# Third and fourth q tiles, and one layer norm, turned by VectorE instead of TensorE

## The chip, the cores and the metric

The kernel runs on one core of a Trainium2 chip. TensorE (PE) multiplies matrices, VectorE (DVE), ScalarE (ACT) and GpSimd (POOL) work on tiles of up to 128 partitions, SyncE (SP) issues the DMA transfers. A tile lies in SBUF; matmuls write to banks of PSUM. The metric is the device time of one execution in microseconds (us), the median of several runs.

## The reference

A transformer block whose layer norms are modulated by a condition `c`, with linear attention and a bilinear FFN. S = 2048 tokens, D = 512, F = 1376, 32 heads of 16:

```python
mod = (silu(c) @ w_mod).reshape(6, D)            # sa, ca, ga, sb, cb, gb
h = layernorm(x) * (1 + ca) + sa
q, k, v = split(h @ wqkv)                        # 32 heads of 16
phi = lambda t: where(t > 0, t + 1, exp(t)) + 1e-6
kv = sum over tokens of phi(k) (x) v             # one 16x16 matrix per head
z = sum over tokens of phi(k)
o = (phi(q) @ kv) / (phi(q) . z + 1e-6)
x = x + ga * (o @ wo)
h = layernorm(x) * (1 + cb) + sb
x = x + gb * (((h @ w_gate) * (h @ w_up)) @ w_down)
```

## The kernel before

The 2048 tokens are four chunks of four tiles of 128 tokens, so tile i is tile j = i mod 4 of chunk i div 4. Every product of fp32 matrices is three matmuls of a shorter type: each operand is split into a high part (ACT copies it) and a low part (the rest, a subtraction on DVE or POOL), and high·high, high·low and low·high are summed in PSUM (`product`, L207 to L209). `split` does this for one tile, `split_raw` for a weight.

The first phase loads the inputs and runs over the 16 tiles with a step i for each: norms, products with the key weights, the sum z and the sum over tokens of x and phi(k). A table `extra` hangs other work on these steps: at steps 4 to 7 the four splits of the value weights, at steps 14 and 15 the splits of the output weight `wo`. Then 48 small matmuls of 128x128 make the key-value matrix, and `w_out` multiplies it with `wo`, so that attention and output projection become one matrix of 512 x 512, the four pairs `wp`.

For a q tile the kernel computes phi(q) with tokens on partitions (`q_a`, `q_b`), its denominators (`den_p` the product with z, `den_r` the sum over a head, `den_b` the constant and the reciprocal for a chunk), and scales phi(q) by them (`den_c`, L700). For the product with `wp` the tile has to be turned, so that features are on partitions. Two ways are in use:

- tiles 0 to 3: `turn_a` (L771), four TensorE transposes of 128x128 into PSUM;
- tiles in `FLIPPED` (4 to 15): their columns are held in another order; `move_out` writes the tile to DRAM, `move_in` reads it back with four DMAs that move blocks of 32 rows, and `turn_v` (L802) turns 32x32 blocks with one VectorE instruction, STREAM_TRANSPOSE.

Both end with `turn_h` (L775, the high part on ACT) and `turn_l` (L779, the low part `xl` on DVE). Then `y_step(i)` runs: TensorE transposes of the next tile if it is turned that way, 12 matmuls of tile i (L832) onto a PSUM bank that ACT seeded with x (`y_seed`, L823), the parts of tile i + 1, the sums for the second norm of tile i − 1 (`y_b`, L250 and L251), and whatever else the call hands it.

When a chunk's four tiles have their y, its second layer norm follows: `rstd_of` (`ve` on DVE, L260; the power on POOL, L263), `nmr_of` (DVE, L267), `xhat` (ACT, L272: the tiles n), and for chunks 0 and 1 `ln2_turn`: 16 TensorE transposes (L293) and the modulation with its parts (L305 to L316). The first norms of some chunks are turned through DRAM and VectorE: `lift_out` (L324), `lift_in` (L332, four DMAs per tile), `lift_turn` (L336), `lift_row` (L341, the modulation), `lift_parts` (L349 to L352).

The FFN's F is cut into 11 slices. The last three, f0, f1 and f2 (f2 is 96 wide), are computed plainly per chunk for chunks 0 and 1: `gate_up` (L915 to L917; its second half multiplies the two and splits the product), `down` (L941 to L943), and `evac` (L902), which adds the result to x. Their weights are loaded by `load_ffn`, nine DMAs issued by SP behind the loop over the q tiles, and prepared by `scale_down` (L882), `split_gu` and `split_down`. The other slices go through `ffn`, which is not touched.

The order of the code is the order of each engine's instructions (`manual_schedule`), and SP's queue holds its DMAs in code order too. SBUF has 94 tile buffers that are used again when a tile is done with, PSUM two pools of four banks.

Of the kernel before, what the change touches and what calls it, by code (L numbers as in the profile page):

```python
# [9 lines left out]
F32R = mybir.dt.float32r  # L10
# [4 lines left out]
P = 128  # L15
# [9 lines left out]
def tile_adaln_block(  # L25
# [51 lines left out]
    def B(tag, shape=(P, D), dt=F32):  # L77

        return T(tiles, tag, shape, dt)
# [4 lines left out]
    def bank():  # L84
        return T(ps_w, "bank")
# [100 lines left out]
    def mod_row(v, pair):  # L186
        ps = row_sum(pair)
        t = consts.tile([P, D], F32, name=f"row{v}")
        nc.scalar.activation(t, ps, AF.Copy)
        return t  # L190


    def split(src, h, l, low=None):
        nc.scalar.activation(h, src, AF.Copy)  # L194
        (low or nc.vector).tensor_tensor(l, src, f32(h), op=ALU.subtract)  # L195

    def split_raw(raw, shape=(P, D), low=None):
        h = B("w", shape, F32R)
        l = B("w", shape, F32R)
        split(raw, h[:raw.shape[0]], l[:raw.shape[0]], low)  # L200
        return h, l

    def product(ps, pairs):

        n = len(pairs)
        for i, ((ah, al), (bh, bl)) in enumerate(pairs):
            nc.tensor.matmul(ps, ah, bh, start=i == 0, stop=False)  # L207
            nc.tensor.matmul(ps, ah, bl, start=False, stop=False)  # L208
            nc.tensor.matmul(ps, al, bh, start=False, stop=i == n - 1)  # L209

    def cut(pair, a, b):
        return pair[0][:, a:b], pair[1][:, a:b]

    FLIPPED = range(4, NCH * NJ)

    def by_block(x):
        return x.rearrange("p (s q i) -> p q s i", q=NQ, i=BL)
# [327 lines left out]
    def mod_part(v, *ks):  # L545
        if 0 in ks:
            accs[v] = B("f")
        mod_acc(accs[v], raw_m[v], ks)

    extra = {4: lambda: (wv.extend(split_raw(r) for r in raw_v[0:1]),),  # L550
             5: lambda: (wv.extend(split_raw(r) for r in raw_v[1:2]),),
             6: lambda: (wv.extend(split_raw(r) for r in raw_v[2:3]), mod_load(2),),
             7: lambda: (wv.extend(split_raw(r) for r in raw_v[3:4]),),
# [3 lines left out]
             11: lambda: (mod_part(3, 3), mod_part(4, 0, 1), rows.update({2: mod_row(2, pairs[2])}), raw_o.extend(load(wo_v[k], "raw") for k in range(2, KD))),  # L557
             12: lambda: (mod_part(4, 2, 3), cols.update({3: col_out(3, mod_col(accs[3], bank()), 0.0)}), mod_load(5)),
             13: lambda: (mod_part(5, 0, 1, 2), cols.update({4: col_out(4, mod_col(accs[4], bank()), 1.0)})),
             14: lambda: (mod_part(5, 3), wo_s.extend(split_raw(x) for x in raw_o[:2])),  # L560
             15: lambda: wo_s.extend(split_raw(x) for x in raw_o[2:])}
    pairs = {}
    q_at = {3: 0, 4: 1, 6: 2, 7: 3, 10: 4}
    ahead = {2: k_ps[2], 3: k_ps[3]}
# [102 lines left out]
    def den_z():  # L667

        nc.vector.reduce_sum(den0, zb.rearrange("p (h i) -> p h i", i=DH), axis=AX.X)
        nc.vector.tensor_scalar(den0, den0, EPS_PHI, EPS_DEN, op0=ALU.mult, op1=ALU.add)  # L670
        nc.vector.tensor_copy(den0q.rearrange("p (q s h) -> p q s h", q=NQ, s=KD),
                              den0.rearrange("p (s q h) -> p q s h", q=NQ, s=KD))

    def den_p(ch, *js, on=None):
        for j in js:
            pzs[ch, j] = B("f")
            (on or nc.gpsimd).tensor_tensor(pzs[ch, j], phq[ch * NJ + j], zq if ch * NJ + j in FLIPPED else zb, op=ALU.mult)
# [12 lines left out]

    def den_b(ch):
        nc.vector.tensor_tensor(dens[ch], dens[ch], (den0q if ch * NJ in FLIPPED else den0).unsqueeze(1).to_broadcast([P, NJ, NH]), op=ALU.add)
        nc.vector.reciprocal(dens[ch], dens[ch])

    def den_c(*tiles):

        for i in tiles:
            ch, j = divmod(i, NJ)
            p3 = phq[i].rearrange("p (h i) -> p h i", i=DH)
            nc.vector.scalar_tensor_tensor(p3, p3, EPS_PHI, dens[ch][:, j].unsqueeze(2).to_broadcast([P, NH, DH]),  # L700
                                           op0=ALU.add, op1=ALU.mult)

    def q_tile(i):
        q_a(i, proj(i, wq))

    wp = []
# [36 lines left out]
    kvp = (B("xh", dt=F32R), B("xl", dt=F32R))  # L743
    kvf = B("n")
    nc.vector.tensor_tensor(kvf.rearrange("p (g c) -> p g c", g=KD), kvps.rearrange("p (g c) -> p g c", g=KD),
                            mask.unsqueeze(1).to_broadcast([P, KD, P]), op=ALU.mult)
    den_p(0, 2, on=nc.vector)
    split(kvf, *kvp)
    den_r(0, 2)
    den_a(0, 3, on=nc.vector)  # L750
    den_b(0)
    q_a(8, ps)
    ps = proj(9, wq)
    q_b(8)
    w_out(0, 1)
    q_a(9, ps)
    den_c(0)
    w_out(2, 3)
    q_b(9)
    q_tile(10)  # L760


    pqs = {}

# [24 lines left out]
    def move_out(*tiles):  # L789

        for i in tiles:
            moved[i] = lift_out(f"moved_{i}", phq.pop(i))
# [17 lines left out]
    def ready(*tiles):  # L810
        den_c(*tiles)
        move_out(*tiles)

    y_banks = []

# [448 lines left out]
    def fill(n):  # L1264
        for _ in range(n):
# [2 lines left out]
    f0, f1, f2 = lone  # L1268
    turn_a(0)
    ps = proj(11, wq)  # L1270
    den_c(1)
    turn_h(0)
    turn_l(0)
    y_seed(0)
    den_c(2)
    q_a(11, ps)
    q_b(10)
    y_step(0, lambda: den_c(3), lambda: q_b(11))
    y_step(1, lambda: den_a(1, 0, on=nc.vector))
    y_step(2, lambda: split_gu(f0, nc.gpsimd))  # L1280
    den_a(1, 1, on=nc.vector)
    y_step(3, lambda: scale_down(f0), turn=False, seed=False)
# [15 lines left out]
    split_down(f0, nc.gpsimd)  # L1298
    ready(7)
    move_in(5)  # L1300
    ln2_turn(0, 0, 1, cast=nc.vector)
    q_b(13)
    ps15 = proj(15, wq, acc_bank)
# [27 lines left out]
    turn_v(7)  # L1331
    g()
    den_a(2, 2, on=nc.vector)
    y_step(5, lambda: den_a(2, 3, on=nc.vector))
    y_step(6, lambda: den_b(2), lambda: ready(8))
    y_step(7, lambda: ready(9), lambda: move_in(8), turn=False, seed=False)
    y_b(7)
    norm2[1].rstd_of()
    ready(10)
    ln2_nx(1)  # L1340
# [152 lines left out]
```

## Time and profile before

| | us |
|---|---|
| runs | 552.09, 552.14, 553.29; median 552.14 |
| profiled execution | 551.79 |
| span of the profiled execution | 550.1 |
| TensorE busy | 544.3 |
| VectorE busy | 378.8 |
| ScalarE busy | 294.2 |
| GpSimd busy | 203.5 |

The span is cut into instructions and DMA transfers, all timed from its start; the 1.7 us between execution and span lie outside it. In a row of the timeline stand the start, the duration, the engine, the line of the kernel, the operation, the tile that it writes, those that it reads, and their shapes; `x4` is a group of four. Brackets give the idle time of the engine before the row, and what ended it. Matmuls overlap, so the start of one to the start of the next is its cost, not its duration.

The work around the change lies in these stretches: the 48 small products from 131.57, the first y step from 151.88, the second norm of chunk 0 from 167.52, gate and up of f0 to f2 with y steps 4 to 7 between 176 and 204, and the down product, the second norm of chunk 1 and y steps 8 and 9 from 204.24 to 219.82.

### The profile page before, as it was taken

The page shows a single profiled execution, that of the slowest core. Times are in us where ns is not written, and L with a number is a line of the kernel's source. Part 1 is how long each engine was busy: PE and PEld are TensorE (multiplying, and loading weights), DVE is VectorE, ACT ScalarE, POOL GpSimd, SP SyncE. Part 2 cuts the span into 40 slices and gives each one's busy share as a digit, 9 for nine tenths or more (in the row PEclk, how much of TensorE's full clock was granted, in tenths as well). Part 3 has the DMA queues.
Part 4 walks back from the last instruction along what each step waited for, and adds up shares of the span by engine and source line. Part 5 has one row for each costly group of instructions (what it writes and reads, how often), then busy time and mean ns, then how long its engine had stood idle before and what let it go on. Part 6 is the DMA issues. An engine that isn't in the chain of part 4 may idle for free.

```text
span 550.1 us, 7373 instructions
## 1 busy us (share of the span) xinstructions
PE 544.3 (99%) x2456; PEld 445.7 (81%) x2456; DVE 378.8 (69%) x618; ACT 294.2 (53%) x543; POOL 203.5 (37%) x206
## 2 busy tenths in 40 slices
PE   8999999999999999999999999999999999999997
PEld 7788788888888878878888888877888888888886
DVE  7897779989987876869766576985444344434444
ACT  3695777647577667467674545454443444444210
POOL 2001010001021200066696566766666646446100
PEclk9999999999999999999999999999999999999999
DMA  8903427310504215755454071790344222200004
GB/s 286 385 17 105 126 98 210 101 53 3 157 1 166 64 38 180 243 165 132 145 133 136 19 212 38 245 295 15 120 135 116 58 57 57 59 19 1 0 1 153
DMA packets 64134, 62.48 MB, mean 114 GB/s; under 512 B 7969, under 2 KB 43041, under 8 KB 64097
## 3 DMA queue, kind: packets, MB, share of 16 engines
q1 hardware_dynamic: 64096, 62.02, 36.4%
q8 instruction: 19, 0.31, 0.2%
q14 instruction: 19, 0.15, 0.1%
HBM read 44.70 MB, written 17.30 MB: 113 GB/s over the span
## 4 chain that ended last, share of the span: by engine, by line
PE 97%; DVE 1%; ACT 0%; issue 0%; DVEq 0%
PE bank L1091 33%; PE acc L832 7%; PE acc L1171 6%; PE acc L1173 6%; PE acc L1172 6%; PE bank L209 5%; PE bank L207 4%; PE bank L208 4%; PE acc L416 3%; PE acc L414 3%; PE acc L415 2%; PE bank L917 2%; PE bank L915 2%; PE bank L916 2%; PE acc L146 2%; PE acc L942 1%
## 5 line engine op out<-in xcount | busy, mean ns | idle before, releaser
L1091 PE MATMUL bank<-h,w 128*128 128x512 f32 (+1 forms) x798 | 184.7, 390 | 0.0
L1091 PEld LDWEIGHTS bank<-h,w 128*128 128x128 f32 (+1 forms) x798 | 148.4, 186 | 33.3 <-ACT bank L1096 0.6
L1096 ACT ACTIVATE bank<-bank 128x512 f32<-128x512 f32 (+1 forms) x38 | 22.2, 583 | 139.6 <-PE bank L1091 139.5
L902 DVE TENSOR_TENSOR x<-acc,x 128x512 f32<-128x512 f32 (+1 forms) x73 | 48.5, 680 | 48.3 <-PE acc L1173 47.7
L1077 POOL TENSOR_TENSOR w<-raw,w 128x256 fp32r<-128x256 f32 (+3 forms) x38 | 40.7, 1071 | 91.8 <-ACT w L1070 91.8
L1171 PE MATMUL acc<-w,kh 128*128 128x512 f32 (+2 forms) x154 | 59.6, 387 | 0.0
L1172 PE MATMUL acc<-w,kh 128*128 128x512 f32 (+2 forms) x154 | 59.6, 387 | 0.0
L1173 PE MATMUL acc<-w,kl 128*128 128x512 f32 (+2 forms) x154 | 59.5, 386 | 0.0
L263 POOL TENSOR_TENSOR rstd<-ve,half 128x2 f32<-128x2 f32 (+1 forms) x12 | 11.7, 978 | 119.3 <-DVE ve L262 66.8
L195 POOL TENSOR_TENSOR w<-raw,w 128x512 fp32r<-128x512 f32 (+1 forms) x25 | 35.0, 1404 | 52.8 <-ACT w L194 52.8
L1077 POOL TENSOR_TENSOR w<-t,w 128x512 fp32r<-128x512 f32 (+1 forms) x38 | 49.2, 1313 | 0.0
L195 DVE TENSOR_TENSOR kl<-u,kh 128x512 fp32r<-128x512 f32 (+1 forms) x38 | 26.4, 735 | 30.5 <-ACT kh L194 30.5
L207 PE MATMUL bank<-w,h 128*128 128x512 f32 x104 | 40.9, 394 | 0.0
L209 PE MATMUL bank<-w,h 128*128 128x512 f32 x104 | 40.9, 393 | 0.0
L208 PE MATMUL bank<-w,h 128*128 128x512 f32 x104 | 40.6, 390 | 0.0
L832 PE MATMUL acc<-w,xh 128*128 128x512 f32 x120 | 37.4, 393 | 0.0
L1150 DVE TENSOR_TENSOR u<-bank,u 128x512 f32<-128x512 f32 (+1 forms) x19 | 13.1, 691 | 31.6 <-PE bank L1091 23.9
L1171 PEld LDWEIGHTS acc<-w,kh 128*128 128x128 f32 (+1 forms) x154 | 28.9, 188 | 6.0
L1172 PEld LDWEIGHTS acc<-w,kh 128*128 128x128 f32 (+1 forms) x154 | 28.9, 188 | 5.9
L1173 PEld LDWEIGHTS acc<-w,kl 128*128 128x128 f32 (+1 forms) x154 | 28.9, 188 | 5.9
L1059 POOL TENSOR_TENSOR t<-raw,t 128x256 f32<-128x256 f32 (+1 forms) x34 | 26.1, 768 | 1.3
L832 PEld LDWEIGHTS acc<-w,xh 128*128 128x128 f32 x120 | 22.2, 188 | 4.6
(216 smaller groups left out, 1115.6 us busy)
## 6 DMA issues: line engine op xcount, KB each, us to landing
raw<-in_w_mod_dram SPq DMA_DIRECT2D x24, 256.0 KB, 3.6
raw<-in_B_w_down_dram SPq DMA_DIRECT2D x20, 256.0 KB, 3.0
raw<-in_B_w_gate_dram SPq DMA_DIRECT2D x36, 128.0 KB, 3.4
raw<-in_B_w_up_dram SPq DMA_DIRECT2D x36, 128.0 KB, 3.6
x<-in_A_x_dram SPq DMA_DIRECT2D x16, 256.0 KB, 5.4
out_dram<-x SPq DMA_DIRECT2D x15, 256.0 KB, 2.7
raw<-in_A_wqkv_dram SPq DMA_DIRECT2D x12, 256.0 KB, 5.4
moved<-h SPq DMA_DIRECT2D x12, 256.0 KB, 2.1
```

The source lines that it names most:

```text
L195: (low or nc.vector).tensor_tensor(l, src, f32(h), op=ALU.subtract)
L207: nc.tensor.matmul(ps, ah, bh, start=i == 0, stop=False)
L208: nc.tensor.matmul(ps, ah, bl, start=False, stop=False)
L209: nc.tensor.matmul(ps, al, bh, start=False, stop=i == n - 1)
L832: nc.tensor.matmul(yps[i], x, y, start=False, stop=k == KD - 1 and x is al, skip_group_check=True)
L902: nc.vector.tensor_tensor(xt[:, a:b], dn[j][:, a:b], xt[:, a:b], op=ALU.add)
L1059: sub = lambda out, x, y: (on or nc.gpsimd).tensor_tensor(out, x, y, op=ALU.subtract)
L1077: sub = lambda out, x, y: (on or nc.gpsimd).tensor_tensor(out, x, f32(y), op=ALU.subtract)
L1091: mm = lambda x, y, **kw: nc.tensor.matmul(ps, x[:, k], y, skip_group_check=True, **kw)
L1171: nc.tensor.matmul(ps, hh[:, a:b], dh[:n, c:d], start=i == 0, stop=False)
L1172: nc.tensor.matmul(ps, hh[:, a:b], dl[:n, c:d], start=False, stop=False)
L1173: nc.tensor.matmul(ps, hl[:, a:b], dh[:n, c:d], start=False, stop=i == len(hs) - 1)
```

## The change

- `FLIPPED` begins at tile 2: tiles 2 and 3 of chunk 0 are held in the other column order, written to DRAM and read back (two DMAs out, eight in), and turned by STREAM_TRANSPOSE; their eight TensorE transposes go. `den_b` takes a part of a chunk, as the two halves of chunk 0 now have constants in different orders. The scalings `den_c` of tiles 2, 3 and 1 are moved ahead of q tile 10 and of the first turn; all ten DMAs stand on SP's queue ahead of the nine loads of `load_ffn`.
- The second norm of chunk 1 goes through DRAM: `xhat_blocks`, four DMAs out and 16 in, four `lift_turn`, four `lift_row` and `lift_parts`, instead of 16 TensorE transposes and `ln2_turn`. `rstd_of` and `nmr_of` come in two parts, for tiles 0 to 2 and for tile 3.
- Y steps 5, 6 and 7 follow y step 4 directly; before, gate and up of f2 stood between 4 and 5. `down(0)` takes f0 and f1 first and f2 after. The low part of f2's down weight is made by POOL.
- Denominators of chunks 2 and 3 come sooner: those of tiles 8 and 9 before the second norm of chunk 0 is turned, those of chunk 3 spread over the stretch up to gate and up of f0 in chunk 1.
- One split of a value weight comes at step 3 instead of 4, and all four splits of `wo` at step 14.

```diff
-    FLIPPED = range(4, NCH * NJ)
+    FLIPPED = range(2, NCH * NJ)
...
-    extra = {4: lambda: (wv.extend(split_raw(r) for r in raw_v[0:1]),),
+    extra = {3: lambda: (wv.extend(split_raw(r) for r in raw_v[0:1]),),
...
-             14: lambda: (mod_part(5, 3), wo_s.extend(split_raw(x) for x in raw_o[:2])),
-             15: lambda: wo_s.extend(split_raw(x) for x in raw_o[2:])}
+             14: lambda: (mod_part(5, 3), wo_s.extend(split_raw(x) for x in raw_o))}
...
-    den_b(0)
+    den_b(0, 0, 2)
+    den_b(0, 2, 4)
...
     den_c(0)
+    ready(2)
+    move_in(2)
     w_out(2, 3)
+    ready(3)
+    den_c(1)
+    move_in(3)
     q_b(9)
     q_tile(10)
...
-    den_c(1)
     turn_h(0)
     turn_l(0)
     y_seed(0)
-    den_c(2)
     q_a(11, ps)
     q_b(10)
-    y_step(0, lambda: den_c(3), lambda: q_b(11))
+    y_step(0, lambda: q_b(11))
+    turn_v(2)
     y_step(1, lambda: den_a(1, 0, on=nc.vector))
+    turn_v(3)
     y_step(2, lambda: split_gu(f0, nc.gpsimd))
...
+    den_a(2, 0, 1, on=nc.vector)
     ln2_turn(0, 0, 1, cast=nc.vector)
...
     g = gate_up(0, f1)
     turn_v(6)
-    den_a(2, 0, on=nc.vector)
+    turn_h(5)
+    turn_l(5)
+    y_seed(5)
     split_down(f1, nc.gpsimd)
     g()
-    y_step(4, lambda: scale_down(f2), lambda: den_a(2, 1, on=nc.vector))
-    g = gate_up(0, f2)
-    split_down(f2)
+    y_step(4, lambda: turn_v(7))
     turn_h(6)
     turn_l(6)
-    y_seed(6)
-    turn_v(7)
+    den_b(2, 0, 2)
+    ready(8, 9)
+    move_in(8, 9)
+    y_step(5, lambda: scale_down(f2))
+    y_step(6, lambda: den_a(2, 2, 3, on=nc.vector))
+    y_step(7, turn=False, seed=False)
+    den_b(2, 2, 4)
+    g = gate_up(0, f2)
+    norm2[1].rstd_of(0, 3)
+    y_b(7)
+    ready(10)
+    norm2[1].nmr_of(0, 3)
+    norm2[1].rstd_of(3, 4)
+    norm2[1].xhat_blocks(0, 1, 2)
+    lifts = [lift_out(f"second_1_{n}", norm2[1].n[n]) for n in range(3)]
+    ready(11)
+    norm2[1].nmr_of(3, 4)
+    norm2[1].xhat_blocks(3)
+    lifts.append(lift_out("second_1_3", norm2[1].n[3]))
+    lifts = [lift_in(x) for x in lifts]
+    move_in(10, 11)
+    den_a(3, 0, 1, on=nc.vector)
+    split_down(f2, nc.gpsimd)
     g()
...
-    take = down(0, ahead={1: (lambda: move_in(9), lambda: ready(11)),
-                          3: (lambda: turned_v(8), lambda: y_seed(8, bank), lambda: move_in(10, 11), lambda: turn_v(9))})
+    for i in (8, 9):
+        turn_v(i)
+        turn_h(i)
+        turn_l(i)
+    lift_turn(0, lifts[0])
+    lift_turn(1, lifts[1])
+    take = down(0, parts=((f0, f1), (f2,)), ahead={6: (lambda: y_seed(8, bank),)})
     take()
-    ln2_turn(1, 0, 1)
-    y_step(8, lambda: turn_v(10))
-    ln2_turn(1, 2, 3)
-    y_step(9, lambda: turn_v(11))
+    y_step(8, turn=False)
+    lift_turn(2, lifts[2])
+    lift_turn(3, lifts[3])
+    den_a(3, 2, on=nc.vector)
+    fs = []
+    for k in range(KD):
+        fs.append(lift_row(k, cb, sb))
+        norm2[1].t[k] = lift_parts(k, fs[k])
+    y_step(9, seed=None)
...
+    turn_v(10)
+    turn_h(10)
+    turn_l(10)
+    y_seed(10)
...
     g = gate_up(1, f0)
-    den_a(3, 0, 1, on=nc.vector)
+    den_a(3, 3, on=nc.vector)
+    den_b(3)
     g()
+    turn_v(11)
     y_step(10)
     g = gate_up(1, f1)
-    den_a(3, 2, 3, on=nc.vector)
-    den_b(3)
     ready(12, 13)
     g()
```

More of the change, by code (lines that the diff above doesn't have):

```diff
@@ L689, in den_a, with den_b @@
             den_r(ch, j)
-    def den_b(ch):
-        nc.vector.tensor_tensor(dens[ch], dens[ch], (den0q if ch * NJ in FLIPPED else den0).unsqueeze(1).to_broadcast([P, NJ, NH]), op=ALU.add)
-        nc.vector.reciprocal(dens[ch], dens[ch])
+    def den_b(ch, a=0, b=NJ):
+        d = dens[ch][:, a:b]
+        nc.vector.tensor_tensor(d, d, (den0q if ch * NJ + a in FLIPPED else den0).unsqueeze(1).to_broadcast([P, b - a, NH]), op=ALU.add)
+        nc.vector.reciprocal(d, d)
     def den_c(*tiles):
@@ L704, in q_tile, with turn_a, turn_h, turn_l @@
         q_a(i, proj(i, wq))
+    pqs = {}
+    tps, yps = {}, {}
+    def turn_a(i):
+        tps[i] = turn_bank[0]()
+        phi = phq.pop(i)
+        for k in range(KD):
+            nc.tensor.transpose(tps[i][:, k * P:(k + 1) * P], phi[:, k * P:(k + 1) * P], ident)
+    def turn_h(i):
+        pqs[i] = (B("xh", dt=F32R), B("xl", dt=F32R))
+        nc.scalar.activation(pqs[i][0], tps[i], AF.Copy)
+    def turn_l(i):
+        h, l = pqs[i]
+        nc.vector.tensor_tensor(l, tps.pop(i), f32(h), op=ALU.subtract)
+    def turn(i):
+        turn_a(i)
+        turn_h(i)
+        turn_l(i)
+    SUMS = (0, 1, 2)
+    moved = {}
+    def move_out(*tiles):
+        for i in tiles:
+            moved[i] = lift_out(f"moved_{i}", phq.pop(i))
+    def move_in(*tiles):
+        for i in tiles:
+            moved[i] = lift_in(moved[i])
+    def turn_v(i):
+        tps[i] = B("f")
+        nc.vector.transpose(tps[i].rearrange("p (s m i) -> p m s i", m=NQ, i=BL),
+                            moved.pop(i).rearrange("p (m s i) -> p m s i", m=NQ, i=BL))
+    def turned_v(i):
+        turn_v(i)
+        turn_h(i)
+        turn_l(i)
+    def ready(*tiles):
+        den_c(*tiles)
+        move_out(*tiles)
     wp = []
@@ L757, in tile_adaln_block @@
     den_c(0)
+    ready(2)
+    move_in(2)
     w_out(2, 3)
+    ready(3)
+    den_c(1)
+    move_in(3)
     q_b(9)
     q_tile(10)
-    pqs = {}
-    tps, yps = {}, {}
-    def turn_a(i):
-        tps[i] = turn_bank[0]()
-        phi = phq.pop(i)
-        for k in range(KD):
-            nc.tensor.transpose(tps[i][:, k * P:(k + 1) * P], phi[:, k * P:(k + 1) * P], ident)
-    def turn_h(i):
-        pqs[i] = (B("xh", dt=F32R), B("xl", dt=F32R))
-        nc.scalar.activation(pqs[i][0], tps[i], AF.Copy)
-    def turn_l(i):
-        h, l = pqs[i]
-        nc.vector.tensor_tensor(l, tps.pop(i), f32(h), op=ALU.subtract)
-    def turn(i):
-        turn_a(i)
-        turn_h(i)
-        turn_l(i)
-    SUMS = (0, 1, 2)
-    moved = {}
-    def move_out(*tiles):
-        for i in tiles:
-            moved[i] = lift_out(f"moved_{i}", phq.pop(i))
-    def move_in(*tiles):
-        for i in tiles:
-            moved[i] = lift_in(moved[i])
-    def turn_v(i):
-        tps[i] = B("f")
-        nc.vector.transpose(tps[i].rearrange("p (s m i) -> p m s i", m=NQ, i=BL),
-                            moved.pop(i).rearrange("p (m s i) -> p m s i", m=NQ, i=BL))
-    def turned_v(i):
-        turn_v(i)
-        turn_h(i)
-        turn_l(i)
-    def ready(*tiles):
-        den_c(*tiles)
-        move_out(*tiles)
     y_banks = []
@@ L1321, in tile_adaln_block @@
     turn_v(6)
-    den_a(2, 0, on=nc.vector)
+    turn_h(5)
+    turn_l(5)
+    y_seed(5)
     split_down(f1, nc.gpsimd)
     g()
-    y_step(4, lambda: scale_down(f2), lambda: den_a(2, 1, on=nc.vector))
-    g = gate_up(0, f2)
-    split_down(f2)
+    y_step(4, lambda: turn_v(7))
     turn_h(6)
     turn_l(6)
-    y_seed(6)
-    turn_v(7)
-    g()
[L1333 to L1340, printed above, removed]
-    take = down(0, ahead={1: (lambda: move_in(9), lambda: ready(11)),
-                          3: (lambda: turned_v(8), lambda: y_seed(8, bank), lambda: move_in(10, 11), lambda: turn_v(9))})
-    take()
-    ln2_turn(1, 0, 1)
-    y_step(8, lambda: turn_v(10))
-    ln2_turn(1, 2, 3)
-    y_step(9, lambda: turn_v(11))
+    den_b(2, 0, 2)
[21 more added lines that the diff above has]
+    split_down(f2, nc.gpsimd)
+    g()
+    for i in (8, 9):
+        turn_v(i)
+        turn_h(i)
+        turn_l(i)
+    lift_turn(0, lifts[0])
+    lift_turn(1, lifts[1])
+    take = down(0, parts=((f0, f1), (f2,)), ahead={6: (lambda: y_seed(8, bank),)})
+    take()
+    y_step(8, turn=False)
[3 more added lines that the diff above has]
+    fs = []
+    for k in range(KD):
+        fs.append(lift_row(k, cb, sb))
+        norm2[1].t[k] = lift_parts(k, fs[k])
+    y_step(9, seed=None)
+    for k in range(KD):
+        nc.sync.dma_start(kept[1][k], fs[k])
+    turn_v(10)
+    turn_h(10)
+    turn_l(10)
+    y_seed(10)
     side.update(plain_side((0, 1)))
```

## The prediction

> **What bounds the kernel now.** First the page's totals, then the busy time by stage, then the timeline of single instructions around each edit.
>
> ```profile
> span 550.1 us, 7373 instructions
> PE 544.3 (99%) x2456; PEld 445.7 (81%) x2456; DVE 378.8 (69%) x618; ACT 294.2 (53%) x543; POOL 203.5 (37%) x206
> PE 97%; DVE 1%; ACT 0%; issue 0%; DVEq 0%
> ```
>
> TensorE (PE) is busy for 99% of the span and carries 97% of the chain that ended last. Time can be gained in two ways only: less work for PE, or the few waits hidden inside its "busy". It can be lost wherever another engine hands PE its operand late.
>
> ```profile
> core 0: us, PE busy (x) PEld busy (x) DVE busy (x) ACT busy (x) POOL busy (x), PEclk, DMA share, GB/s
> 148.60:164.20 15.60, 15.60 (x77) 12.88 (x76) 12.80 (x20) 12.37 (x28) 2.18 (x2) 1.00 0.01 2
> 164.20:176.80 12.60, 12.60 (x65) 10.57 (x64) 8.59 (x16) 8.74 (x16) 3.54 (x3) 1.00 0.41 131
> 176.80:204.20 27.40, 27.40 (x123) 21.91 (x122) 24.39 (x39) 18.51 (x38) 3.98 (x3) 1.00 0.17 55
> 204.20:219.80 15.60, 15.60 (x77) 12.96 (x77) 9.27 (x17) 12.09 (x21) 1.39 (x1) 1.00 0.56 187
> ```
>
> These four stages (busy us by engine) hold the y steps of chunk 0, its second norm, the FFN up to y step 7, and the second norm of chunk 1. The granted clock is 1.00 in all of them, so the clock takes no part. VectorE (DVE) is the next bound: 82% busy in the first stage and 89% in the third. The change gives it more work.
>
> **The change part by part.** All times below are the profiled execution's: 551.79 us, of which the span is 550.1; it stands 0.35 under the median of the runs shown, 552.14.
>
> *Transposes taken from PE.* Rows of PE: start, duration, line, operation.
>
> ```profile
> 155.09 0.60 PE L771 MATMUL bank<-ident,h 128*128 128x128 f32 x4
> 158.28 0.60 PE L771 MATMUL bank<-ident,h 128*128 128x128 f32 x4
> 187.80 0.62 PE L832 MATMUL acc<-w,xh 128*128 128x512 f32 x2
> 190.52 0.39 PE L915 MATMUL bank<-h,w 128*96 128x512 f32 x1
> 212.48 1.04 PE L293 MATMUL bank<-ident,n 128*128 128x128 f32 x8
> 216.11 1.03 PE L293 MATMUL bank<-ident,n 128*128 128x128 f32 x8
> 219.82 0.39 PE L915 MATMUL bank<-h,w 128*128 128x512 f32 x1
> ```
>
> A y step with four transposes takes 158.28 − 155.09 = 3.19; one without, 190.52 − 187.80 = 2.72. So each q tile that PE no longer turns gives 0.47, two give 0.94. Eight norm transposes and a y step take 216.11 − 212.48 = 3.63 and then 219.82 − 216.11 = 3.71; less 2.72 that is 0.91 and 0.99. The 24 transposes are worth **−2.84**, about 0.12 each. [...]
>
> *Weight splits sooner (wo at step 14, wv[0] at step 3).* Rows of PE and DVE:
>
> ```profile
> 131.57 0.22 PE L207 MATMUL bank<-w,w 128*128 128x128 f32 x1
> 133.22 0.28 PE L207 MATMUL bank<-w,w 128*128 128x128 f32 x1
> 137.24 0.68 PE L183 MATMUL bank<-w,ones_r 128*128 128x512 f32 x2
> 130.41 2.49 DVE L195 TENSOR_TENSOR w<-n,w 128x512 fp32r<-128x512 f32 x4
> ```
>
> The key-value product has 48 small matmuls. The first 12 took 133.22 − 131.57 = 1.65, the other 36 took 4.02, or 0.112 each; 12 at that pace are 1.34, so 0.31 is waiting, for the four low parts of `tt` that DVE ends at 132.90. Two wo lows (half of 2.49) go ahead of that point into earlier idle time, so the wait should go: **−0.31**. If DVE has no idle time there, it stays: 0.
>
> *First y step.* Rows of PE and DVE:
>
> ```profile
> 152.78 0.40 PE L832 MATMUL acc<-w,xl 128*128 128x512 f32 x1
> 150.65 0.68 DVE L700 SCALAR_TENSOR_TENSOR h<-h,den 128x512 f32<-128x512 f32 x1
> 151.24 0.68 DVE L779 TENSOR_TENSOR xl<-bank,xh 128x512 fp32r<-128x512 f32 x1
> ```
>
> PE's third matmul of y 0 (152.78) wants xl(0), which is ready at 151.24 + 0.68 = 151.92: 0.86 to spare. The change puts the scaling of q tiles 2 and 3 (den_c, one every 0.60, from 150.65 to 151.24) ahead of it: 1.20 − 0.86 = **+0.34**. Den_b in halves adds instructions of under 0.3 beside it, left in the bounds. If DVE's idle time before these takes one scaling, the term is 0; if both halves of den_b count, +0.6.
>
> *First chunk's second norm.* Rows of DVE, ACT, PE, SP's queue, and from the table of DMA issues (the last three; last column: us from issue to landing; the row of w_down is for 136 to 143):
>
> ```profile
> 161.48 0.68 DVE L882 TENSOR_TENSOR raw<-raw,row 128x512 f32<-128x512 f32 x1
> 162.08 1.79 DVE L677 TENSOR_TENSOR f<-h,z 128x512 f32<-128x512 f32 x1
> 167.52 0.11 DVE L260 TENSOR_SCALAR ve<-sums 128x4 f32<-128x4 f32 x1
> 169.43 2.94 ACT L272 ACTIVATE n<-x,nmr,rstd 128x512 f32<-128x512 f32 x4 [1.03 <-DVE nmr L267]
> 172.38 1.03 PE L293 MATMUL bank<-ident,n 128*128 128x128 f32 x8
> 136.32 0.38 SPq L113 DMA_DIRECT2D raw<-in_B_w_gate_dram  x1
> 137.35 0.45 SPq L113 DMA_DIRECT2D raw<-in_B_w_down_dram  x1
> 79.53 7.49 SPq L332 DMA_DIRECT2D u<-first  x16
> raw<-in_B_w_down_dram SPq DMA_DIRECT2D x2, 256.0 KB, 5.4
> moved<-h SPq DMA_DIRECT2D x12, 256.0 KB, 2.1
> u<-moved SPq DMA_DIRECT2D x48, 64.0 KB, 2.1
> ```
>
> The two outs and eight ins of q tiles 2 and 3 stand on SP's queue ahead of the nine FFN weight loads, so the loads, which began at 136.32, now wait for tile 3. Its scaling ends near 151.0 (DVE's frame is 0.3 earlier there with PE); +2.1 for the out, +1.9 for four ins at 7.49 / 16 = 0.47, +1.03 from the gate load to the down load, +5.4 to landing: 161.4, with two issue steps of some 0.1 about 161.6. scale_down(f0), which began at 161.48, waits for it: +0.15. The two new STREAM_TRANSPOSEs (1.4) fit in the 15.60 − 12.80 = 2.8 in which DVE had nothing to do. Everything behind scale_down on DVE up to ve (167.52) moves with it, then rstd on POOL, nmr, the four n's on ACT (ready at 172.37). PE wants the fourth n with its fourth transpose, 0.36 after 172.38, so 0.37 was to spare. PE arrives 0.94 + 0.31 − 0.34 = 0.91 sooner than before, the n's 0.15 later: 0.91 + 0.15 − 0.36 = **+0.70**. That is, what PE gained up to here is nearly all given back. Bounds: 0 if DVE moves ahead as PE does; +1.3 if the load lands 0.6 later.
>
> *Tiles 5 to 8 in a row.* Each y step of 2.72 has a STREAM_TRANSPOSE (0.71 by the row 209.07 below), a low (0.60) and a denominator (two at 0.60 to 0.68) for DVE: 2.6. That just fits: 0, bound +0.65 for one operation stretched as the one at 162.08 is (1.79 for 0.68). The low of f2's down weight, now on POOL, takes one operation from DVE here; on POOL it stands behind both halves of chunk 1's rstd, so it holds up nothing that a norm waits for.
>
> *Second chunk's second norm.* Rows of DVE, PE, ACT and DVE, then a DMA issue:
>
> ```profile
> 209.07 0.71 DVE L802 STREAM_TRANSPOSE f<-u 128x512 f32<-128x512 f32 x1 [0.67 <-DMA u<-moved]
> 212.56 2.44 DVE L902 TENSOR_TENSOR x<-acc,x 128x512 f32<-128x512 f32 x4
> 204.24 0.39 PE L941 MATMUL acc<-w,kh 128*128 128x512 f32 x1
> 62.83 0.82 ACT L341 ACTIVATE f<-wide,col,col 128x512 f32<-128x512 f32 x1 [3.91 <-DVE wide L336]
> 64.34 0.69 DVE L352 TENSOR_TENSOR h<-f,h 128x512 fp32r<-128x512 f32 x1 [1.55 <-ACT h L351]
> u<-stowed SPq DMA_DIRECT2D x8, 256.0 KB, 4.7
> ```
>
> PE starts the down products near 204.05 (204.24, less the 0.2 gained by the terms so far), then has 36 down matmuls at 0.227 (8.17) and y 8 and y 9 (5.44): it wants the first operand of gate_up(1,f0) at 217.7, its low part 0.23 later, 217.9. DVE's chain from there: copy, multiply, high and low of the last g, at 0.6 to 0.69 each (from PE's last result near 204.4 to 207.1); two turned tiles, each 0.71, ACT's high 0.6 and the low 0.69, 2.05 with the steps between (211.2); two lift_turns (212.4); four evacuations (2.44: 214.8); two lift_turns (216.05); then row 0, its high and its low (64.34 + 0.69 − 62.83 = 2.2 in the first norm): 218.25. **+0.35**. The 16 ins: the n's are out near 204.0, so the last in is issued at 204.3 + 7.5 = 211.8 and landed at 213.9, ahead of the fourth lift_turn at 215.4. Bounds: 0 to +1.0 (one stretched operation).
>
> *One answer.* Denominators of chunk 3 sooner, turns of tiles 10 and 11, stores of the norm after their rows: DVE and SP work beside PE, 0. SP issues 30 DMAs more (10 for tiles 2 and 3, 20 for the norm), 14 us of its queue, spread over stages with a DMA share of at most 0.56.
>
> Sum: −2.84 − 0.31 + 0.34 + 0.70 + 0.35 = −1.76.
>
> **The rivals.** *Whole gain:* the orders leave no new wait. For it: the added waits are all under 0.8, sums of a dozen rows each; a DVE operation or two less on a chain ends them. −3.15: 549.0 by the median.
>
> *VectorE eats the gain.* The three chains end on DVE, whose operations go from 0.68 to 1.79 at 162.08. One such stretch of 0.65 more at each place: 550.4 + 1.95 = 552.35; without any gain beyond that, "no change". Against it: POOL is busy for only 2 to 4 us of each stage. [...]
>
> *Slower: lift-ins in series.* If the 16 ins of the second norm take buffers that come free only as the tile before is turned, each group of four costs 1.87 of issue and 2.1 of landing: 204.3 + 4 × 3.97 = 220.2, against 215.4 wanted: +4.8, 555.2. It decides from +3.4 on, a landing at 218.8. For it: loads through DRAM of 256 KB took 4.7 (u<-stowed). Against it: the first norm's 16 were issued in 7.49 without a gap, and landed in 2.1.
>
> **How the numbers follow.** Profile 551.79 − 1.76 = 550.03; the median stood 0.35 above: **550.4**. About 0.3% (1.66 us) is what a measurement of this kernel can tell from no change, so the bound is 550.5. My forecast, own range 549.7 to 551.1, has 0.45, of which 0.28 lies under the bound; the whole gain (549.0 to 549.7) 0.24; VectorE eats the gain (551.1 to 552.4) 0.18; slower 0.13. Faster 0.52, same 0.35, slower 0.13. Range 548.9 (the fastest run, 552.09, less 3.15) to 552.4.
>
> **What would show it.** PE would have 24 instructions fewer in L771 and L293's lines; no pause within the 48 small products; a pause of some 0.3 before the third matmul of y 0; the first L293 group with a wait of 0.7 behind ACT's n; y 5 to 7 at 2.72 each; a wait of 0.3 at gate_up(1,f0) behind a low part. Wrong would be: weights of f0 that land after 163, a y step over 3.0 between 187 and 205, or lift-ins that land after 215.4.

## The result

The changed kernel takes **550.3 us** (median of 7 runs, 549.82 to 551.05); the kernel before, run beside it, 552.14. The ratio is 0.9965 (95% interval 0.9955 to 0.9974): faster by 0.35%. The forecast was 550.4.

The page of the changed kernel:

```profile
span 549.3 us, 7400 instructions
PE 542.7 (99%) x2432; PEld 444.3 (81%) x2432; DVE 382.7 (70%) x631; ACT 293.1 (53%) x541; POOL 206.4 (38%) x208
PE 94%; DVE 2%; ACT 1%; DMA 1%; SPq 1%; issue 0%; POOL 0%; DVEq 0%; POOLq 0%
```

PE has 24 instructions fewer, DVE 13 more. The chain that ended last now has 6% off PE, twice as much as before: it leaves PE where PE waits.

The profiled execution took 550.99, one of the longer ones. The window from 10 to 20 us says why. The kernel before (busy us by engine, then granted clock, DMA share, GB/s):

```profile
10.00:20.00 10.00, 10.00 (x60) 8.29 (x60) 8.68 (x19) 8.30 (x14) 0.00 (x0) 1.00 1.05 388
```

The changed kernel:

```profile
10.00:20.00 10.00, 9.59 (x50) 7.84 (x51) 8.72 (x19) 8.30 (x14) 0.00 (x0) 0.83 1.04 389
```

In this execution the granted clock stood at 0.83 there, and the first three-matmul product (L207) began at 39.08 for 37.67 before: 1.4 us were lost long before the first line that the change makes slower or faster (the split of the value weight, on DVE at 55.81). Executions of either kernel lie over 1 us apart. So traces are compared from the first of the 48 small products on. The timeline of PE, with one row of its weight loads (PEld), changed kernel:

```profile
132.75 0.22 PE L207 MATMUL bank<-w,w 128*128 128x128 f32 x1
138.06 0.68 PE L183 MATMUL bank<-w,ones_r 128*128 128x512 f32 x2
149.54 0.65 PE L714 MATMUL bank<-ident,h 128*128 128x128 f32 x4
150.14 0.19 PEld L207 LDWEIGHTS bank<-w,h 128*128 128x128 f32 x1 [0.18 <-DVE n L765]
150.14 0.50 PE L207 MATMUL bank<-w,h 128*128 128x512 f32 x1
153.40 0.66 PE L714 MATMUL bank<-ident,h 128*128 128x128 f32 x4 [0.25 <-DVE h L376]
154.36 0.40 PE L838 MATMUL acc<-w,xl 128*128 128x512 f32 x1
172.99 0.49 PE L293 MATMUL bank<-ident,n 128*128 128x128 f32 x3
173.84 0.77 PE L293 MATMUL bank<-ident,n 128*128 128x128 f32 x5 [0.35 <-ACT n L272]
174.36 0.47 PE L207 MATMUL acc<-w,h 128*128 128x512 f32 x1
189.00 0.62 PE L838 MATMUL acc<-w,xh 128*128 128x512 f32 x2
199.89 0.39 PE L921 MATMUL bank<-h,w 128*96 128x512 f32 x1
205.43 0.39 PE L947 MATMUL acc<-w,kh 128*128 128x512 f32 x1
219.10 0.39 PE L921 MATMUL bank<-h,w 128*128 128x512 f32 x1
219.32 0.40 PE L922 MATMUL bank<-h,w 128*128 128x512 f32 x1
```

With the same points of the kernel before, and what each step changed (us):

| point on PE | before | changed | step | forecast |
|---|---|---|---|---|
| first small product | 131.57 | 132.75 | | |
| transposes of tile 0 | 148.66 | 149.54 | −0.30 | −0.31 |
| first matmul of y 0 | 152.23 | 153.82 | +0.71 | +0.34 (in y 0) |
| first matmul behind y 3 | 164.21 | 164.82 | −0.98 | −0.94 |
| behind the first norm group | 173.16 | 174.36 | +0.59 | +0.70 |
| y 4 | 187.80 | 189.00 | 0.00 | 0 |
| down products | 204.24 | 205.43 | −0.01 | 0 |
| gate_up(1,f0) | 219.82 | 219.10 | −1.91 | −1.90 + 0.35 |
| the stretch | 88.25 | 86.35 | **−1.90** | −1.76 |

From gate_up(1,f0) to the end both take 330.2 to 330.3. Everything that the change gained up to the first norm (−0.30 − 0.98) is lost at two waits (+0.71 + 0.59); what is left is the second norm's 16 transposes.

Both waits are kept by other engines. DVE, then ACT, of the changed kernel:

```profile
147.60 1.29 DVE L700 SCALAR_TENSOR_TENSOR h<-h,den 128x512 f32<-128x512 f32 x2
148.80 1.28 DVE L765 TENSOR_TENSOR n<-bank,row 128x512 f32<-128x512 f32 x2
151.46 1.29 DVE L700 SCALAR_TENSOR_TENSOR h<-h,den 128x512 f32<-128x512 f32 x2
152.66 0.69 DVE L376 SCALAR_TENSOR_TENSOR h<-bank,h 128x512 f32<-128x512 f32 x1
153.26 0.68 DVE L722 TENSOR_TENSOR xl<-bank,xh 128x512 fp32r<-128x512 f32 x1
157.64 0.69 DVE L722 TENSOR_TENSOR xl<-f,xh 128x512 fp32r<-128x512 f32 x1 [0.70 <-ACT xh L718]
162.30 0.69 DVE L682 TENSOR_REDUCE den<-f 128x32 f32<-128x512 f32 x1
162.91 0.68 DVE L888 TENSOR_TENSOR raw<-raw,row 128x512 f32<-128x512 f32 x1
163.50 1.78 DVE L676 TENSOR_TENSOR f<-h,z 128x512 f32<-128x512 f32 x1
216.21 0.71 DVE L336 STREAM_TRANSPOSE wide<-u 128x512 f32<-128x512 f32 x1 [0.21 <-DMA u<-second]
218.47 0.69 DVE L352 TENSOR_TENSOR h<-f,h 128x512 fp32r<-128x512 f32 x1 [0.26 <-ACT h L351]
170.85 2.93 ACT L272 ACTIVATE n<-x,nmr,rstd 128x512 f32<-128x512 f32 x4 [1.84 <-DVE nmr L267]
```

The low part of tile 0 was ready at 153.26 + 0.68 = 153.94, before the third matmul of y 0 (154.36) wanted it. What PE waited for was a PSUM bank, twice. The product of q tile 11 came 0.24 late (0.60 behind the transposes of tile 0, for 0.36 before): the bank that it writes was held until the second multiply of `w_out(2, 3)` ended, at 150.08 ([0.18 <-DVE n L765]), with the scaling of tile 2 now ahead of it (the second of the two at 147.60). The transposes of tile 1 came 0.41 late ([0.25 <-DVE h L376]): their bank was held until the addition of q tile 9 ended, at 153.35, with the scalings of tiles 2, 3 and 1 ahead of it (those of 3 and 1 at 151.46). The norm waits for the fourth n, ready at 170.85 + 2.93 = 173.78.

### The profile page after: what moved, and what is told of

It reads as the page before. It is cut to its first block, busy times and chain, and to the rows that moved or that the text cites. A ratio compares the mean times of both kernels' runs of the same rounds, so it can differ in the third digit from the quotient of the medians.

```text
span 549.3 us, 7400 instructions
## 1 busy us (share of the span) xinstructions
PE 542.7 (99%) x2432; PEld 444.3 (81%) x2432; DVE 382.7 (70%) x631; ACT 293.1 (53%) x541; POOL 206.4 (38%) x208
## 4 chain that ended last, share of the span: by engine, by line
PE 94%; DVE 2%; ACT 1%; DMA 1%; SPq 1%; issue 0%; POOL 0%; DVEq 0%; POOLq 0%
PE bank L1097 33%; PE acc L1177 6%; PE acc L1178 6%; PE acc L1179 6%; PE acc L838 5%; PE bank L209 5%; PE bank L207 5%; PE bank L208 4%; PE acc L416 3%; PE acc L414 3%; PE acc L415 3%; PE bank L921 2%; PE bank L923 2%; PE bank L922 2%; PE acc L948 1%; PE acc L947 1%
## 5 line engine op out<-in xcount | busy, mean ns | idle before, releaser
L195 POOL TENSOR_TENSOR w<-raw,w 128x512 fp32r<-128x512 f32 (+1 forms) x26 | 36.7, 1415 | 56.4 <-ACT w L194 52.2
L263 POOL TENSOR_TENSOR rstd<-ve,half 128x2 f32<-128x2 f32 (+3 forms) x13 | 12.6, 970 | 113.0 <-DVE ve L262 67.4
L207 PE MATMUL bank<-w,h 128*128 128x512 f32 x104 | 40.9, 394 | 0.0
```

## The experiments

Every kernel below is the changed kernel with one edit more. "Stretch" is the time from the first small product to the first matmul of gate_up(1,f0) in its profile: 86.35 for the changed kernel, 88.25 before. Ratios are to the kernel before, run beside it (its medians 552.1 to 552.6). A stretch is read from one execution. How well it repeats shows behind the first norm group: from there to gate_up(1,f0) the changed kernel and the eight others whose edits leave that part alone took 44.71 to 44.74. The stretch ahead, from the product at 39.08 to the first small product, repeats less well: kernels with the same code there took 93.66 to 94.26.

**Q tiles 2 and 3 back to TensorE.**

```diff
-    FLIPPED = range(2, NCH * NJ)
+    FLIPPED = range(4, NCH * NJ)
...
     den_c(0)
-    ready(2)
-    move_in(2)
     w_out(2, 3)
-    ready(3)
-    den_c(1)
-    move_in(3)
     q_b(9)
...
+    den_c(1)
     turn_h(0)
     turn_l(0)
     y_seed(0)
+    den_c(2)
...
-    y_step(0, lambda: q_b(11))
-    turn_v(2)
+    y_step(0, lambda: den_c(3), lambda: q_b(11))
...
-    turn_v(3)
```

> The changed kernel with q tiles 2 and 3 turned by TensorE again, and the denominators of chunk 0 in the order of before; all else as changed. Theory: the two tiles give 0.94 on TensorE, and the same edit brings two waits, 0.65 at the first y step (for PSUM banks that VectorE frees later) and 0.59 at the transposes of chunk 0's second norm (for the last n); together 1.24, so this part of the change loses 0.3. Expected: 0.3 faster than the changed kernel, 550.0. From the first of the 48 small products to the first matmul of gate_up(1,f0) the changed kernel took 219.10 - 132.75 = 86.35; expected here 86.1. Rival: each tile gives its 0.47 and the waits come from elsewhere: 0.9 slower than the changed kernel, 551.2 (87.3 for the stretch).

550.09 (ratio 0.9964, 0.9952 to 0.9975), stretch 132.95 to 218.88, 85.93. So this part of the change gains nothing: the stretch is 0.42 shorter without it, and the runs, as good as equal, exclude the rival's 0.9. Neither wait is there any more (3.56 from the transposes of tile 0 to y 0, and 0.79 for the first norm group, for 3.57 and 0.78 before the change). Eight transposes fewer on PE came with two waits that cost more.

**The second norm of chunk 1 back to TensorE.**

```diff
-    norm2[1].xhat_blocks(0, 1, 2)
-    lifts = [lift_out(f"second_1_{n}", norm2[1].n[n]) for n in range(3)]
+    norm2[1].xhat(0, 1, 2)
...
     take()
+    ln2_turn(1, 0, 1)
     y_step(8, turn=False)
-    lift_turn(2, lifts[2])
-    lift_turn(3, lifts[3])
     den_a(3, 2, on=nc.vector)
-    fs = []
-    for k in range(KD):
-        fs.append(lift_row(k, cb, sb))
-        norm2[1].t[k] = lift_parts(k, fs[k])
+    ln2_turn(1, 2, 3)
...
```

> The changed kernel with the second norm of chunk 1 transposed by TensorE again (16 transposes, no transfers through DRAM), the order of y steps and all else as changed. Theory: this part is the whole net gain. 16 transposes at 0.12 come back: 1.9 slower than the changed kernel, 552.2; the stretch from the first small product to gate_up(1,f0) 86.35 + 1.87 = 88.2. Rival: some of the gain of the changed order is in the rows, and the norm through DRAM pays for its own waits: under 1.0 slower, 551.3.

552.59 (1.0003, 0.9992 to 1.0013): the whole gain is gone. The stretch is 132.77 to 221.35, 88.58, of which 1.79 lie behind the down products, as expected, and 0.45 at the first norm, where DVE's scale_down waited 0.37 for its weight in this execution.

**GpSimd's split of f0 out of DVE's way.**

```diff
-    y_step(2, lambda: split_gu(f0, nc.gpsimd))
+    y_step(2)
...
     norm2[0].rstd_of()
+    split_gu(f0, nc.gpsimd)
```

> The changed kernel with the split of f0's gate and up weights (ScalarE highs, GpSimd lows) put behind the reciprocal root of chunk 0's second norm; nothing else is moved. Theory: the two products of VectorE that took 1.78 and 1.06 beside GpSimd's 3 us go back to 0.68 each, the chain to the last n is 1.5 shorter, and the wait of 0.59 in the first group of norm transposes goes: 0.6 faster than the changed kernel, 549.7. Rival: the products were long for another reason, or the n's wait for the sums of the fourth y: no change, 550.3. Second rival: the lows come too late for gate_up(0,f0), slower.

551.25 (0.9977, 0.9967 to 0.9987), stretch 87.02: no gain, 0.67 longer. Rows of DVE, then PE:

```profile
161.70 0.69 DVE L888 TENSOR_TENSOR raw<-raw,row 128x512 f32<-128x512 f32 x1 [0.31 <-DMA raw<-in_B_w_down_dram]
162.31 0.69 DVE L676 TENSOR_TENSOR f<-h,z 128x512 f32<-128x512 f32 x1
167.98 1.25 DVE L267 SCALAR_TENSOR_TENSOR nmr<-sums,rstd 128x4 f32<-128x4 f32 x1 [0.30 <-POOL rstd L263]
179.48 1.82 DVE L316 TENSOR_TENSOR h<-f,h 128x512 fp32r<-128x512 f32 x1
181.36 0.50 PE L922 MATMUL bank<-h,w 128*128 128x512 f32 x1 [0.33 <-DVE h L316]
```

The products are 0.69 again, so it was GpSimd that made them 1.78: its two lows stand beside them from 163.44 to 166.44 in the changed kernel, and from 167.92 to 170.47 here. But nmr, with four elements per partition and 0.16 in the changed kernel, now took 1.25 beside the same lows, so even an instruction with almost no data was lengthened, and a low part of the norm beside the next ones (179.46 to 182.45; 1.82 for 0.69) came late for gate_up(0,f0). The first row of DVE shows the other limit of this chain: scale_down waited 0.31 for f0's weight.

**Late reads.**

```diff
-    lifts = [lift_in(x) for x in lifts]
     move_in(10, 11)
+    lifts = [lift_in(x) for x in lifts]
```

> The changed kernel with the eight reads back of tiles 10 and 11 put ahead of the sixteen reads back of chunk 1's second norm on the DMA queue. It puts a price on late reads. Theory: in the changed kernel the fourth lift_turn waited 0.21 for its transfer and gate_up(1,f0) had 0.16 to spare, so the reads are at the edge already; eight issues took 4.49, and nearly all of it reaches TensorE: 4.3 slower, 554.6. Rival: the transfers are hidden with room, no change.

554.16 (1.0031, 1.0019 to 1.0043), stretch 90.09: 3.74 longer, near the 4.3. The place was another one. Rows of DVE and PE, then windows:

```profile
215.52 0.71 DVE L336 STREAM_TRANSPOSE wide<-u 128x512 f32<-128x512 f32 x1 [2.88 <-DMA u<-second]
217.49 0.73 PE L838 MATMUL acc<-w,xh 128*128 128x512 f32 x2 [1.80 <-ACT acc L829]
```

```profile
212.78:217.49 4.71, 2.91 (x13) 2.07 (x11) 1.97 (x4) 0.60 (x1) 0.00 (x0) 1.00 0.43 108
217.49:222.00 4.51, 4.51 (x13) 3.49 (x13) 4.22 (x7) 2.12 (x4) 0.00 (x0) 0.62 0.21 68
```

The second lift_turn held up the evacuations behind it on DVE, these the bank of y 9, and PE waited there. The wait is about 2.0; the rest, 1.7, is that y 9 took 221.94 − 217.49 = 4.45 for 2.72, at a granted clock of 0.62. So late reads do reach PE, as the slower rival of the prediction said, and at a price near the one given; but here they were issued late, while the rival had them wait for buffers, which no run shows. The fourth lift_turn of the changed kernel already waits 0.21 for its transfer.

**Weight splits back.**

```diff
-    extra = {3: lambda: (wv.extend(split_raw(r) for r in raw_v[0:1]),),
+    extra = {4: lambda: (wv.extend(split_raw(r) for r in raw_v[0:1]),),
...
-             14: lambda: (mod_part(5, 3), wo_s.extend(split_raw(x) for x in raw_o))}
+             14: lambda: (mod_part(5, 3), wo_s.extend(split_raw(x) for x in raw_o[:2])),
+             15: lambda: wo_s.extend(split_raw(x) for x in raw_o[2:])}
```

> The changed kernel with the weight splits where they were: value weight 0 at step 4, the last two of wo at step 15. Theory: the wait of 0.31 among the 48 small products comes back, and it moves VectorE's chain to the norm as well, so it is not absorbed there: the stretch from the first small product to gate_up(1,f0) 86.35 + 0.3 = 86.65, and 0.2 more before it, where the two steps after value weight 0's split were 0.2 shorter: 550.8. Rival: TensorE arrives late at a norm that waits for VectorE anyway, so nothing changes, 550.3 (86.35).

550.93 (0.9977, 0.9964 to 0.999), stretch 131.65 to 218.32, 86.67: the 0.3 is back and is not absorbed by the norm. Whether the earlier part is 0.2 longer can't be told: from the product at 39.08 to the first small product the changed kernel took 93.67, this one 93.76 and the kernel before 93.90, all within the 93.66 to 94.26 of kernels with the same code there.

**The first y step's order.**

```diff
     den_c(0)
-    ready(2)
-    move_in(2)
-    w_out(2, 3)
-    ready(3)
-    den_c(1)
-    move_in(3)
-    q_b(9)
+    w_out(2, 3, between=lambda: (ready(2), move_in(2)))
+    q_b(9)
+    den_c(1)
+    ready(3)
+    move_in(3)
```

(`between` runs between the multiplies and the splits of `w_out`.)

> The changed kernel with another order of VectorE before the first y step: den_c(2) between the multiplies and the low parts of w_out(2,3), then the q tile 9 addition, den_c(1) and only then den_c(3). Theory: the two waits for PSUM banks (0.24 and 0.41) fall to some 0.2 together, but den_c(3), and behind it on the DMA queue the reads of tile 3 and the weights of f0, come 1.2 later. scale_down(f0) then waits some 1.0 for its weight, the four n's come 1.0 later, and TensorE loses there what it won and 1.0 more: 551.3, the stretch from the first small product to gate_up(1,f0) 87.3. Rival: TensorE's waits count where they are, 0.45 faster: 549.85 (85.9).

551.27 (0.9988, 0.9974 to 1.0002), so the median is where it was expected; the profiled execution was a long one (552.88), stretch 89.32. Y 0 began without the two waits, as meant. Rows of DVE and PE, then windows:

```profile
162.52 1.69 DVE L887 TENSOR_TENSOR raw<-raw,row 128x512 f32<-128x512 f32 x1 [0.61 <-DMA raw<-in_B_w_down_dram]
171.95 0.33 PE L293 MATMUL bank<-ident,n 128*128 128x128 f32 x1 [0.37 <-ACT n L272]
174.07 1.33 PE L293 MATMUL bank<-ident,n 128*128 128x128 f32 x5 [0.38 <-ACT n L272]
```

```profile
174.07:179.10 5.03, 5.03 (x18) 4.22 (x19) 3.97 (x8) 2.91 (x5) 1.28 (x1) 0.66 0.76 226
175.00:179.10 4.10, 4.10 (x15) 3.29 (x14) 3.08 (x6) 2.01 (x4) 1.28 (x1) 0.69 0.82 258
```

scale_down waited for the weight and then ran beside GpSimd (1.69 for 0.68); PE now waited for each n in turn, and was given a clock of 0.69 behind it: the next 12 matmuls took 3.98 for 2.83. Taking away the first wait made the kernel slower than the changed one by its median (551.27 for 550.3; the intervals of the two ratios touch), as the chain through SP's queue says.

**The chain to the first norm shortened.** GpSimd's lows and scale_down go behind nmr, the highs stay (`highs_gu` and `lows_gu` are the two halves of `split_gu`):

```diff
-    y_step(2, lambda: split_gu(f0, nc.gpsimd))
+    y_step(2, lambda: highs_gu(f0))
...
-    y_step(3, lambda: scale_down(f0), turn=False, seed=False)
+    y_step(3, turn=False, seed=False)
...
     ln2_nx(0)
+    scale_down(f0)
+    lows_gu(f0)
```

> The changed kernel with VectorE's chain to chunk 0's second norm shortened: GpSimd's lows of f0's gate and up (the highs stay) and scale_down(f0) are put behind nmr. Theory: in the run with the whole split put behind the reciprocal root the two products fell from 1.78 and 1.06 to 0.69, but nmr beside GpSimd took 1.25 for 0.16 and the low before gate_up(0,f0) 1.82; here nothing of GpSimd stands beside the chain, and scale_down's 0.6 is out of it. The n's are 2.1 earlier, the wait of 0.59 goes: 549.7, the stretch from the first small product to gate_up(1,f0) 85.8. Rival: the lows are now late for gate_up(0,f0), a wait of the same size there: 550.3 (86.35).

549.94 (0.9956, 0.9939 to 0.9972), stretch 132.20 to 217.94, 85.74. The first norm group of PE has no wait any more:

```profile
172.43 1.03 PE L293 MATMUL bank<-ident,n 128*128 128x128 f32 x8
```

The 0.59 was this chain. (nmr, at 168.01, still took 1.25 beside GpSimd, which began its lows at 167.95; the chain now has room for it.)

**Both together.** The order of the first y step with the shortened chain, and

```diff
-    y_step(0, lambda: q_b(11))
-    turn_v(2)
+    y_step(0, lambda: turn_v(2), lambda: q_b(11))
```

> The order of VectorE before the first y step of the run before last, with the shortened chain, and the turn of tile 2 ahead of the q tile 11 addition. Theory: with the weight of f0 off the chain to the norm, the waits for PSUM banks count: both gains add, 0.6 + 0.45, 549.25, the stretch from the first small product to gate_up(1,f0) 85.3. Rival: tile 3, read back 1.2 later, holds up y 3 by as much as the first y step gains: 549.7 (85.8).

551.37 (0.9982, 0.9971 to 0.9993), stretch 87.49. Both theories missed the size; the rival had the place. DVE and PE:

```profile
160.80 0.71 DVE L745 STREAM_TRANSPOSE f<-u 128x512 f32<-128x512 f32 x1 [2.69 <-DMA u<-moved]
162.71 0.50 PE L837 MATMUL acc<-w,xh 128*128 128x512 f32 x1 [1.91 <-ACT acc L828]
```

DVE waited 2.69 for tile 3, and PE 2.07 at y 3. With the order of the first y step alone, the same reads had cost DVE 0.28; they were issued from 155.26 here and from 155.01 there, as the last thing on SP's queue ahead of the nine loads. The median of the four from issue to landing was 1.9 in both runs, and the first load behind them took 4.2 here and 4.1 there, so neither tells the two apart. Why tile 3 came that late here and not there isn't shown.

**Banks from the other pool.** The order stays; the product of q tile 11 and the turned tile 1 take banks of the other PSUM pool, first alone, then with the shortened chain. These two kernels, by the author's inference, leave out part of the addition of x to one y tile (the relative error of their output is 0.0206); their times can be read.

```diff
-    ps = proj(11, wq)
+    ps = proj(11, wq, acc_bank)
...
+    turn_bank[0] = acc_bank
     y_step(0, lambda: q_b(11))
+    turn_bank[0] = bank
```

> The changed kernel with two tiles of PSUM taken from the other pool: the product of q tile 11 and the turned tile 1. The order of every engine is as changed. Theory: the waits of 0.24 and 0.41 before the first y step were for banks that VectorE frees late, so they go, but for some 0.25 in which the third matmul of y 0 waits for its low part; yet TensorE then only arrives 0.4 sooner at the norm that ends 0.59 too late for it, so nothing is gained: 550.3, the stretch from the first small product to gate_up(1,f0) 86.35, its wait in the first norm group 1.0. Rival: the waits count, 0.4 faster: 549.9 (85.95).

551.01 (0.9972, 0.996 to 0.9984), stretch 132.32 to 218.76, 86.44: no gain (what the median has above 550.3 lies outside the stretch, which is 0.09 longer). Y 0's two waits for banks are gone, its third matmul now waits 0.24 for the low part, and the norm takes back the rest. PE:

```profile
172.27 0.38 PE L293 MATMUL bank<-ident,n 128*128 128x128 f32 x2
173.53 0.77 PE L293 MATMUL bank<-ident,n 128*128 128x128 f32 x5 [0.38 <-ACT n L272]
174.05 0.48 PE L207 MATMUL acc<-w,h 128*128 128x512 f32 x1
```

From 172.27 to 174.05 is 1.78 for a group of 0.78: a wait of 1.0, as expected.

> The same two banks, with VectorE's chain to the norm shortened as in the run that put GpSimd's lows and scale_down(f0) behind nmr. Theory: with the chain short, TensorE's earlier arrival counts: 0.4 less than that run, 549.55, the stretch from the first small product to gate_up(1,f0) 85.3. The n's are then ready 0.2 to 0.3 after TensorE wants the first but before the fourth. Rival: as in the run with another order, something else of the early part comes late, no gain: 549.95 (85.75).

549.7 (0.995, 0.9936 to 0.9964), stretch 133.10 to 218.56, 85.46: 0.28 less than with the short chain alone. The same edit that was worth nothing counts once the wait behind it is gone.

**Three products moved instead.** With the short chain, the turned tiles in their own pool:

```diff
-    ps = proj(9, wq)
+    ps = proj(9, wq, acc_bank)
...
-    q_tile(10)
+    q_a(10, proj(10, wq, acc_bank))
...
-    ps = proj(11, wq)
+    ps = proj(11, wq, acc_bank)
```

> As the run before it, with the chain to the norm shortened, but now the products of q tiles 9, 10 and 11 are put into the other PSUM pool, and both turned tiles stay in their own; so no accumulated y tile follows a turned one in its bank. [...] Theory: the two waits for banks are gone here as well, without the early work being moved: 549.55, the stretch from the first small product to gate_up(1,f0) 85.4, with some 0.3 of waiting left before the third matmul of y 0. Rival: the three products now wait for banks that the sums over x free late, no gain: 85.75 or more.

**548.98** (0.9937, 0.9925 to 0.995), stretch 131.51 to 217.00, 85.49. This version beats both kernels. Of the 1.3 that its median is below the changed kernel's the stretch shows 0.86.

**The low part first.** The same, with q_b(9) behind turn_l(0):

```diff
-    q_b(9)
...
     turn_l(0)
+    q_b(9)
     y_seed(0)
```

> The same, with the q tile 9 addition of VectorE put behind the low part of tile 0 (its bank is no longer wanted soon). Theory: the low part is 0.6 earlier, the last wait before y 0 goes, and as the chain to the norm has room, TensorE keeps it: 0.3 less, 549.25, the stretch from the first small product to gate_up(1,f0) 85.1. Rival: the n's of the norm become the bound again, no change to the run beside it, 85.4.

549.02 (0.9937, 0.9924 to 0.9951), stretch 132.66 to 217.80, 85.14: 0.35 less, as expected, but the runs don't tell it from the one before, and some of it is on loan. DVE and PE:

```profile
215.25 0.71 DVE L336 STREAM_TRANSPOSE wide<-u 128x512 f32<-128x512 f32 x1 [0.54 <-DMA u<-second]
218.25 0.50 PE L933 MATMUL bank<-h,w 128*128 128x512 f32 x1
```

The second matmul of gate_up(1,f0) is at 218.25, 0.45 after the first for 0.23: DVE's fourth lift_turn waited 0.54 for its transfer, and the low part came at 218.20. The prediction's wait at this place appears once PE comes early enough.

## Why the prediction was right, and where it was not

- **24 transposes, −2.84.** Right: −0.98 for eight, −1.91 at the second norm for 16, −2.89 in all; the experiment with the second norm gives 1.79 back for its 16. Turning on VectorE pays for the norm and, as the changed kernel stands, not for q tiles 2 and 3 (0.42 lost by the stretch); with the chain short and the banks moved the q tiles seem to pay too (85.14 to 85.49 against 85.93, for a kernel that keeps them on TensorE and has no wait at these two places; it was not run with these edits).
- **Weight splits, −0.31.** Right: −0.30, and 0.32 by undoing it.
- **First y step, +0.34.** The step "PE's third matmul of y 0 wants xl(0)" failed. Scalings of VectorE were the cause, but they struck earlier, through two PSUM banks given back late (0.24 behind tile 2's, 0.41 behind those of tiles 2, 3 and 1); the wait for xl(0) itself was nothing. Measured +0.71. The working had followed operands and had not asked which instruction frees the bank that PE writes next. With the banks moved, the low part's wait came up, as 0.24, and it went when the low part was put first.
- **First norm, +0.70.** Size and place right (+0.59), the working only in part. Counted from the first small product PE came 0.57 sooner than before, not 0.91, as it had lost more in y 0; the fourth n came 0.23 later, not 0.15. "The two new STREAM_TRANSPOSEs fit in the 2.8 in which DVE had nothing to do" was wrong: behind each, DVE waits 0.70 for ACT's high part in order, and is not late for scale_down by the load but by its own queue (162.91, straight behind the row before). In the executions with 0.31 and 0.37 of waiting there, the load was late as well; the two limits lie close together.
- **Tiles 5 to 8 in a row, 0.** Right: 199.89 − 189.00 = 10.89, four steps of 2.72.
- **Second norm, +0.35.** Mis-sized: 0. The low part ended at 218.47 + 0.69 = 219.16, the second matmul wanted it at 219.32. Relative to the first small product PE was 0.2 later than forecast there, and DVE's chain 0.27 shorter.
- **The sum.** Two misses, of 0.37 too little and 0.35 too much, cancel; −1.76 against −1.90. That the median came out 0.1 from the forecast is in part luck: it owes something to that, and to medians of executions that lie over 1 us apart.
- **The rivals.** "VectorE eats the gain" is what happened at the first two places, and only there; it did so by the order of VectorE's queue, not by newly stretched operations (the one of 1.78 took 1.79 before). The slower one did not happen. In the changed kernel the low part is ready 0.16 before gate_up(1,f0) wants it; once reads came late they cost 3.74, near the price given, though at y 9 and not at gate_up(1,f0).

What stays open: why some executions lose over 1 us at the start, how much the earlier value weight gives, and why the reads of tile 3 landed late in the run with both edits.

## What to carry to other kernels

Follow a removed matmul to the next point where TensorE waits for a chain of another engine: what was gained before it is worth nothing until that chain is shorter, and then it is worth all of it (the same two banks bring PE 0.29 earlier to the norm: worth nothing, then 0.28). Ask of each instruction put into a queue not only which operand it delays but which buffer it keeps from being freed, and what stands behind it on the DMA queue. A small time that agrees with the forecast can be two errors that cancel, so compare term by term, from a point behind the noise of the start.

## What the runs showed of the hardware

- In two runs a wait of TensorE cost more than itself. After a wait of 1.96 (late reads) the granted clock was 0.62 over the next 4.51 us, which added 1.7; after four waits of 0.4 in a row (first y step's order) it was 0.66 over the next 5.03 us, and the 12 matmuls behind that group took 1.15 more. In the late reads' y 9 matmuls stood 0.43 apart for 0.227, near half speed; at the start of the changed kernel the granted clock was 0.50 from 16.20 to 19.40. An estimate from these numbers, for a clock of 0.50: the slow stretches lasted 2 × 0.38 × 4.51 = 3.4, 2 × 0.34 × 5.03 = 3.4 and, at the start of the changed kernel, 2 × 0.17 × 10.00 = 3.4 us. After 2.07 in the run with both edits the clock stayed at 1.00 (162.70 to 166.00). What decides whether it falls isn't shown.
- In the two kernels with the turned tile 1 in the accumulation pool the output has a relative error of 0.0206; with the same product moved but the turned tiles left in their pool it was not there. That part of the addition of x is missing in the y tile that came next in tile 1's bank is the author's inference; no run shows the bank itself.
